# Nine more seven-product steps, state additions and rT on GpSimd, and a reordered head in a fused SSD and gated-cosine kernel

## The chip, the cores and the metric

The kernel runs on one core of one Trainium2 chip. The metric is the device time of one execution in microseconds (us). A core has five engines with a queue each, which run their own instructions in order and wait for one another by semaphores: TensorE (PE; its weight loads are shown as PEld), VectorE (DVE), ScalarE (ACT), GpSimd (POOL) and SyncE (SP), which here issues nearly all transfers. Matrix products go to PSUM; GpSimd works on SBUF alone in this kernel.

## The reference

Two stages, all in fp32. The first is a state-space scan (Mamba-2 SSD) over 4 sequences, 8 heads, 768 positions, head width D = 32 and state width N = 16. In chunks of positions:

```python
cum = cumsum(log(clip(a)))                      # within the chunk
L   = exp(cum_i - cum_j), causal
M   = (C_i . B_j) * L
y   = M @ x + (C_i . state) * exp(cum_i)
state = exp(sum(la)) * state + sum_j B_j x_j exp(cum_last - cum_j)
```

The second takes the result as 3072 tokens of width 256 through a gated layer of width 2048:

```python
h = x @ w_in          # 3072x256 @ 256x2048
g = h * cos(h)
out = g @ w_out       # 3072x2048 @ 2048x256
```

## The kernel before

**Blocks and steps.** Positions are cut into 6 blocks c of 128; two units of 64 positions make a block. The result of the scan for a block, yT, has 512 columns: 256 per unit u. The layer on top runs in 96 steps n, 16 per block (n = 16c + f). In blocks 1 to 5 steps f = 0 to 7 belong to unit 0 and f = 8 to 15 to unit 1; j counts the 8 pieces of the layer's width within a unit. A step consists of:

- the first product hp = yT x w_in on PE (`first`, line 672), 8 passes of 256 columns;
- `wind_k` (ACT, 679), `wind_w` (DVE, 685), `gate` (ACT sine, 694) and `gated` (DVE, 699), which make gT = h cos h out of hp;
- `differ` (GpSimd, 724 to 727): three operations that make the sums and differences gd of gT;
- the second product (`second`, `seven`, 848) into o, two steps later (LAG = 2).

The second product is done in Strassen-Winograd form from block 1 on: seven products of half size for eight, with operands gd and the prepared weight differences (`differ_w`). After the eight steps of a unit the seven partial sums are copied (`take`, ACT), added up and stored (`rest`, 873); `unsummed` spreads the four parts of that over four steps on GpSimd.

**Runs.** In some steps, the *runs*, the first product takes that form too (`first7`, 772): 7 products of two passes of 128 columns, i.e. 14 passes, in the order 1, 6, 7, 5, 4, 3, 2. It needs differences of y (`differ_y`, 754, four of them, i = 0 to 3, in the tile `yd`, which lies in `ms[2]`) and of w_in (`differ_in`, 743). Product 6 reads difference 2, products 5, 7 and 4 read differences 0, 1 and 3. Difference 2 is made of difference 0. The sums of a seven-product step are made on DVE (785 to 793), and `gated` of the step before a run stands behind the sums of its first step. Runs before: steps 41 to 45, 57 to 61 and 73 to 77 (f = 9 to 13 of blocks 2 to 4), and 81 to 93. PSUM for the running sums and one hp comes from the tag "scan", two buffers of two banks, which the scan also uses.

**The scan of a block.** It is laid out over the steps of the block before it, in the table `steps`: `reaches` (running products of a, 586), `turn_blocks` (a transpose on DVE, 594), `turn2` (ACT copies of C scaled, 603, and rT = C times reach, DVE, 605), `inner2` (products g, 615), `weights` (477), `add_state` (state of the block before, decayed and added, 510), `decays0` (running products for the block after next, 387), `open2` and `finish2` (the y products, 629 and 641), and ACT copies of y to yT (`take_y`). `differ_y` of unit 1 is made by GpSimd at f = 4, 5, 6, 6. In the loop over n the work of a step is recorded in the order: first product, wind, take_y, gate, the first item of the list `behind`, gated with differ, the rest of `behind`, differ_y, sums of the outputs, differ_in, second product, inner2. This order is the order in each engine's queue.

**The head.** Blocks 0 and the first units are done unit by unit (`inner`, `weights`, `finish0`, `reach0`, `weigh_c`). Up to the first product at 14.47 us C must be loaded (`load_c`, four transfers on ACT's queue), copied (358), transposed (407) and scaled (411); B transposed (421); a spread over heads (`spread_a`, 376) and scanned (387). hp 0 is done in two halves; between them stands the whole of `finish0(1)`: the rT products (527), the sums for the state (489) and the y products (537). The weights come in pieces as 32-bit words, are graded (`grade`: ACT 256, 258, GpSimd 259) and joined (`join`: DVE 271, 275, GpSimd 283).

## Time and profile before

| | |
|---|---|
| median of 3 runs | 364.44 us (363.73 to 365.11) |
| profiled execution | 364.44 us |
| its span, first to last instruction | 362.7 us |
| mean granted TensorE clock | 0.998 |
| L672, first products, 544 passes | 129.6 us, 382 ns each |
| L724, 726, 727, gd on GpSimd, 79 each | 735, 501, 493 ns |
| L754, differ_y on GpSimd, 128x128, 12 of them | 455 ns |
| L510, state additions on DVE, 28 of them | 419 and 754 ns |
| L605, rT on DVE, 8 of them | 507 ns |
| L586, reach scans on DVE, 32 of them | 368 ns |

The passes overlap each other, so the time of one pass (382 ns) is longer than the distance from one to the next. A line number is that of the kernel before; a tile's name stands left of the arrow, what it is made of on the right.

### The profile page before, as it was taken

Reading aid. Unit: us, or ns where it says so; the run is one execution under the profiler, and the core shown is the slowest. Engines: PE = TensorE matmul, PEld = TensorE weight load, DVE = VectorE, ACT = ScalarE, POOL = GpSimd, SP = SyncE. Lnnn points to the kernel's source line nnn. Section 1 sums busy time; section 2 is a strip of 40 time slices with the busy share of each in tenths; the row PEclk is TensorE's granted clock in tenths of the full one; section 3 lists DMA queues with packets and bytes.
Section 4 is the critical chain, followed back from the end, with each engine's and each line's share of the span. In section 5 each row is a group of like instructions: output and inputs, shape, how many; then the busy total and the mean of one; then the engine's idle time right before and its main releaser. Section 6 shows DMA issues by size and latency. Waiting matters only on the chain.

```text
span 362.7 us, 10240 instructions
## 1 busy us (share of the span) xinstructions
PE 357.0 (98%) x4070; PEld 326.0 (90%) x4070; DVE 276.0 (76%) x504; ACT 184.0 (51%) x352; POOL 239.7 (66%) x387
## 2 busy tenths in 40 slices
PE   8999999999999999999999999999999999999995
PEld 4788888889999999999989999999999999999995
DVE  7779998488876987878766877875776776688864
ACT  3597656544454346534536533545553544444552
POOL 5567767699666677674786666686666465475572
PEclk9999999999999999999999999999999999999999
DMA  7984997666583429113228202110001001001001
GB/s 138 246 284 141 189 196 122 85 125 98 134 129 58 99 51 135 14 34 76 53 53 119 23 3 75 28 33 11 0 2 31 0 3 33 0 3 29 3 17 44
DMA packets 96624, 26.43 MB, mean 73 GB/s; under 512 B 86624, under 2 KB 92480, under 8 KB 96576
## 3 DMA queue, kind: packets, MB, share of 16 engines
q1 hardware_dynamic: 95328, 25.38, 34.9%
q8 instruction: 32, 0.52, 0.6%
q10 hardware_dynamic: 1248, 0.39, 0.5%
q14 instruction: 16, 0.13, 0.1%
HBM read 22.36 MB, written 3.34 MB: 71 GB/s over the span
## 4 chain that ended last, share of the span: by engine, by line
PE 96%; DMA 2%; DVE 1%; issue 0%; ACT 0%; POOL 0%; DVEq 0%
PE o L848 35%; PE hp L672 33%; PE o L808 8%; PE m L772 7%; PE hp L772 5%; DMA bc<-in_C_dram 2%; PE y L641 2%; PE g L615 1%; PE y L489 1%; PE y L629 1%; PE g L468 1%; PE y L537 1%; PE y L527 1%; PE o L900 0%; PE tp L451 0%
## 5 line engine op out<-in xcount | busy, mean ns | idle before, releaser
L672 PE MATMUL hp<-yT,w_in 128*128 128x256 f32 x544 | 129.6, 382 | 0.1
L672 PEld LDWEIGHTS hp<-yT,w_in 128*128 128x128 f32 x544 | 99.0, 190 | 13.8 <-issue 1.4
L724 POOL TENSOR_TENSOR gd<-gT 128x256 f32<-128x256 f32 x79 | 58.1, 735 | 76.9 <-DVE gT L699 61.8
L694 ACT ACTIVATE w<-w,quarter 128x512 f32<-128x512 f32 x96 | 69.4, 723 | 65.8 <-DVE w L685 65.7
L685 DVE SCALAR_TENSOR_TENSOR w<-hp,k 128x512 f32<-128x512 f32 x96 | 65.8, 686 | 45.4 <-ACT k L679 45.2
L679 ACT ACTIVATE k<-hp 128x512 int32<-128x512 f32 x96 | 57.2, 596 | 68.6 <-PE hp L672 60.3
L699 DVE TENSOR_TENSOR gT<-hp,w 128x512 f32<-128x512 f32 x96 | 65.6, 683 | 12.2 <-ACT w L694 8.3
L848 PE MATMUL o<-words,gd 128*128 128x128 f32 x474 | 66.0, 275 | 0.0
L848 PEld LDWEIGHTS o<-words,gd 128*128 128x128 f32 x474 | 59.4, 192 | 0.0
L848 PE MATMUL o<-w_out,gT 128*128 128x128 f32 x316 | 50.4, 278 | 0.0
L848 PEld LDWEIGHTS o<-w_out,gT 128*128 128x128 f32 x316 | 45.4, 191 | 3.1
L726 POOL TENSOR_TENSOR gd<-gT,gd 128x128 f32<-128x128 f32 x79 | 39.6, 501 | 6.2
L727 POOL TENSOR_TENSOR gd<-gT,gd 128x128 f32<-128x128 f32 x79 | 39.0, 493 | 6.2
L848 PE MATMUL o<-w_out,gd 128*128 128x128 f32 x158 | 30.6, 276 | 0.0
L848 PE MATMUL o<-words,gT 128*128 128x128 f32 x158 | 30.6, 275 | 0.0
L808 PE MATMUL o<-w_out,gT 128*128 128x256 f32 x128 | 30.0, 380 | 0.0
L387 DVE TENSOR_TENSOR_SCAN lam<-arow,unit 128x512 f32<-128x512 f32 x20 | 29.9, 1496 | 0.1
L808 PEld LDWEIGHTS o<-w_out,gT 128*128 128x128 f32 x128 | 24.2, 190 | 3.6 <-POOL w_out L283 0.4
L848 PEld LDWEIGHTS o<-words,gT 128*128 128x128 f32 x158 | 24.0, 192 | 0.0
L848 PEld LDWEIGHTS o<-w_out,gd 128*128 128x128 f32 x158 | 24.0, 192 | 0.0
L772 PE MATMUL m<-m,words 128*128 128x128 f32 x168 | 23.4, 276 | 0.0
L772 PE MATMUL hp<-yT,w_in 128*128 128x128 f32 x112 | 21.7, 275 | 0.0
(130 smaller groups left out, 463.6 us busy)
## 6 DMA issues: line engine op xcount, KB each, us to landing
words<-in_moe_w_in_dram SPq DMA_DIRECT2D x8, 512.0 KB
words<-in_moe_w_out_dram SPq DMA_DIRECT2D x8, 512.0 KB
xr<-in_x_dram SPq DMA_DIRECT2D x24, 128.0 KB
arow<-a_cut SPq DMA_DIRECT2D x10, 256.0 KB
arow<-a_cut SPq DMA_DIRECT2D x10, 252.0 KB
out_dram<-sum SPq DMA_DIRECT2D x18, 128.0 KB
bc<-in_B_dram SPq DMA_DIRECT2D x24, 64.0 KB
blocks<-in_B_dram SPq DMA_DIRECT2D x16, 32.0 KB
```

The source lines that it names most:

```text
L387: V.tensor_tensor_scan(out=lams[k][:, p, hs].rearrange(flat), data0=rows_.rearrange(flat), data1=unit0[:, hs].rearrange(flat), initial=0.0 ...
L672: PE.matmul(to_[:, e], lhsT=w_in[:, k, fs], rhs=y[:, k], start=(k == 0), stop=(k == KT - 1), skip_group_check=True)
L679: ACT.activation(k, hp[n], AF.Copy, bias=0.25, scale=INV_2PI)
L685: V.scalar_tensor_tensor(out=w, in0=hp[n], scalar=INV_2PI, in1=k, op0=ALU.mult, op1=ALU.subtract)
L694: ACT.activation(cos, cos, AF.Sin, bias=quarter, scale=TWO_PI)
L699: V.tensor_tensor(out=gT[n], in0=hp.pop(n), in1=cos, op=ALU.mult)
L724: G.tensor_tensor(out=d[:, 0:2], in0=g[:, 1:2].to_broadcast([P, 2, P]), in1=g[:, 3::-3], op=ALU.subtract)
L726: G.tensor_tensor(out=d[:, 2], in0=g[:, 0], in1=d[:, 0], op=ALU.subtract)
L727: G.tensor_tensor(out=d[:, 3], in0=g[:, 2], in1=d[:, 2], op=ALU.subtract)
L772: PE.matmul(dst[q], lhsT=w[q], rhs=y_[q], start=(q in (6, 1, 7)), stop=True, skip_group_check=True)
L808: PE.matmul(o[c, u][:, t], lhsT=g[:, 2 * e + t], rhs=w_out[:, 2 * j + e], start=(j == e == t == 0), stop=(j == NJ - 1 and e == 1), skip_gr ...
L848: PE.matmul(at[q], lhsT=a_[q], rhs=w[q], start=(j == 0 and q in starts), stop=(j == NJ - 1), skip_group_check=True)
```

## The change

Runs are added at f = 2, 3, 4 of blocks 2, 3 and 4 (steps 34 to 36, 50 to 52, 66 to 68). The scan's work on DVE is moved away from these steps: reaches to f = 5 as two scans of 260 elements for eight of 64 (the rows are stored with a leading zero, `lead` starts each run of 65), the block transposes to the last step of the block before and f = 1, the first `decays0` from f = 2 to f = 0. rT becomes a function of its own, `scale2`, on GpSimd for blocks 3 to 5, and so does the state addition, `add_state2`, two operations for four. The copies of C (`turn2`) stay on ACT at f = 3 and 4. `differ_y` makes both units' differences at f = 0, 0, 1, 1 on GpSimd. The sums of the outputs keep out of f = 2 and 3 on GpSimd.

In the head the fourth C transfer goes to SP's queue behind the load of a; the copy of C is one GpSimd operation; C is transposed ahead of B; x of unit 1 is loaded ahead of the second weight piece; the first piece is joined in halves; in `finish0` of units 0 and 1 the sums stand ahead of the y products; half of g of unit 1 is done behind the first half of hp 0.

```diff
@@ load_c, loads @@
-    for b in range(NB):
-        load_c(b, nc.scalar)
+    for i in range(NB):
+        load_c(i, nc.scalar if i < NB - 1 else nc.sync)
...
-    fetch("in", 1)
     for s in range(2):
         load_x(1, s)
+    fetch("in", 1)
@@ join @@
+            if halves:
+                for f in (slice(0, P), slice(P, 2 * P)):
+                    G.tensor_tensor(out=dst[:, :, f].bitcast(U32), in0=bits[:, :, f],
+                                    in1=last[:, :, f], op=ALU.add)
+                return
@@ add_state, now beside it @@
+    def add_state2(k):
+
+        dec = scan.tile([P, 2, 2, 2 * D], FP32, tag="whole", bufs=1, name="whole")
+        flat = "p s q d -> p (s q) d"
+        G.tensor_tensor(out=dec.rearrange(flat), in0=after[k - 1].rearrange(flat),
+                        in1=reach[k // 2][:, :, k % 2, W:].to_broadcast([P, NB, 2 * D]),
+                        op=ALU.mult)
+        return lambda: G.tensor_tensor(out=after[k], in0=after[k], in1=dec, op=ALU.add)
@@ finish0 @@
+        if k < 2:
+            sums(k, at, strip, start=True)
+        if between:
+            between()
...
-        sums(k, [y[0][:, s, 3 * P:] for s in range(2)], lambda q, s: slice(32 * q, 32 * q + 32),
-             start=(k == 0))
+        if k > 1:
+            sums(k, at, strip)
@@ reaches @@
-    def reaches(c, b):
-        s, p = divmod(b, 2)
-        if p == 0:
-            reach[c, s] = scan.tile([P, 2, P], FP32, tag="reach", name="reach")
-        for k in range(2):
-            i = slice(k * W, (k + 1) * W)
-            V.tensor_tensor_scan(out=reach[c, s][:, p, i], data0=along[c][:, b, i],
-                                 data1=ones[:, 0:W], initial=1.0, op0=ALU.mult, op1=ALU.mult)
+    def reaches(c, s):
+        if s == 0:
+            reach[c] = scan.tile([P, NB, 2, W + 1], FP32, tag="reach", bufs=1, name="reach")
+        V.tensor_tensor_scan(
+            out=reach[c][:, 2 * s:2 * s + 2].rearrange("p b k i -> p (b k i)"),
+            data0=along[c][:, 2 * s:2 * s + 2].rearrange("p b i -> p (b i)"),
+            data1=lead.rearrange("p b i -> p (b i)"), initial=0.0, op0=ALU.mult, op1=ALU.add)
@@ turn2 @@
-        rT = scan.tile([P, 2, P], FP32, tag="rT", name="rT")
-        V.tensor_tensor(out=rT, in0=tp[:, 1], in1=reach[c, s], op=ALU.mult)
-        part[c, s] = (tp[:, 0], cT, rT)
+        part[c, s] = (tp[:, 0], cT)
+
+    def scale2(c, s, eng):
+        r2[c, s] = rT = scan.tile([P, 2, P], FP32, tag="rT", name="rT")
+        eng.tensor_tensor(out=rT.rearrange("p q (k i) -> p q k i", k=2),
+                          in0=turned.pop((c, s))[:, 1].rearrange("p q (k i) -> p q k i", k=2),
+                          in1=reach[c][:, 2 * s:2 * s + 2, :, 1:], op=ALU.mult)
@@ head, in order @@
     tp_b = bank([P, 4, P], "tp", "o")
+    take_c, of_c = turn_c()
+    take_c(0)
     turn_b(0, tp_b)()
-    ACT.copy(out=c0[:, 3:4].rearrange("p r h n -> p h r n"), in_=c4[:, :, 3:4])
...
-    join("in", 0)
+    c1 = copy_c(of_c)
+    join("in", 0, halves=True)
     decays0(1, 0, 1, 2)
+    yT0, take_s0, _ = finish0(0, lambda: spread_a(1, 1, tag="h"))
     decays0(1, 1)
-    take_s0, _ = finish0(0)
-    take_b = turn_b(1, tp_b)
+    weigh0(1)
+    turn_b(1, tp_b)()
     scan_reach = reach0(1)
     scan_reach()
-    take_b()
+    weigh_c(1, c1)
+    yT0()
     take_s0()
-    for t in range(2):
-        inner(1, t)
-    weigh0(1)
-    weigh_c(1, of_c)
+    inner(1, 0)
@@ first_steps @@
-        for q in range(2):
-            weights(1, q)
+        weights(1, 0)
         states_of = []
-        first(0, lambda: states_of.extend(finish0(1)))
+
+        def unit1():
+            inner(1, 1)
+            weights(1, 1)
+            states_of.extend(finish0(1))
+
+        first(0, unit1)
@@ steps @@
-             dict(reach=(1, 2), turn=(3, 4), inner=5, weigh=(6, 7), state=(0, 5),
-                  decays=(2, 8, 14, 15), along=(6, 7)) for c in range(2, NC)}
+             dict(reach=(5, 5), turn=(-1, 1), cut=(3, 4), scale=(6, 7), inner=5, weigh=(6, 7),
+                  state=(2, 8), decays=(0, 8, 14, 15), along=(6, 7)) for c in range(2, NC)}
@@ runs @@
-    runs = [*(range(NF * c + 9, NF * c + 14) for c in range(2, NC - 1)),
+    runs = [*(range(NF * c + f, NF * c + l) for c in range(2, NC - 1) for f, l in ((2, 5), (9, 14))),
             range(NC * NF - 15, NC * NF - 2)]
@@ the loop over n @@
-            for i, at in enumerate((4, 5, 6, 6) if 2 <= c < NC - 1 else ()):
+            for i, at in enumerate((0, 0, 1, 1) if 2 <= c < NC - 1 else ()):
                 if at == f:
-                    differ_y(c, i, G, slice(1, 2))
-            if unsummed and (c > 1 or summed[0]):
+                    differ_y(c, i, G)
+            for e, s in chunks_at(n, "scale"):
+                if e > 2:
+                    scale2(e, s, G)
+            for add in adds:
+                add()
+            adds[:] = [add_state2(2 * e - 1 + i) for e, i in chunks_at(n, "state") if e > 2]
+            if unsummed and (c > 1 and f not in (2, 3) or summed[0]):
```

More of the change, by code (lines that the diff above doesn't have):

```diff
@@ L77 @@
     along, blocks = {}, {}
-    ones = const.tile([P, P], FP32, name="ones")
-    V.memset(ones, 1.0)
+    lead = const.tile([P, NB, W + 1], FP32, name="lead")
     def fill(dst):
@@ L87, in fill @@
                   start=True, stop=True, skip_group_check=True)
-    a_all = dram.tile([NB, H, S], FP32, name="a_all")
+    a_all = dram.tile([NB, H, 2 * NC, W + 1], FP32, name="a_all")
     a_cut = dram.tile([NB, H, S], FP32, name="a_cut")
@@ L177, in load_unit_along @@
                 nc.sync.dma_start(
-                    out=alongs[k][:, 2 * p + s, 1:],
-                    in_=a_all[2 * s + p, :, k * W:(k + 1) * W].unsqueeze(1).to_broadcast([H, N, W]))
+                    out=alongs[k][:, 2 * p + s],
+                    in_=a_all[2 * s + p, :, k].unsqueeze(1).to_broadcast([H, N, W + 1]))
     def load_along(c, seqs=range(NB)):
@@ L185, in load_along @@
         if c not in along:
-            along[c] = rows.tile([P, NB, P], FP32, tag="along", bufs=2, name="along")
+            along[c] = rows.tile([P, NB, 2 * (W + 1)], FP32, tag="along", bufs=2, name="along")
         for b in seqs:
@@ L191, in load_along @@
                 nc.sync.dma_start(
-                    out=along[c][rs, b], in_=a_all[b, hs, c * P:(c + 1) * P].unsqueeze(1)
-                    .to_broadcast([hs.stop - hs.start, N, P]))
+                    out=along[c][rs, b], in_=a_all[b, hs, 2 * c:2 * c + 2]
+                    .rearrange("h k i -> h (k i)").unsqueeze(1)
+                    .to_broadcast([hs.stop - hs.start, N, 2 * (W + 1)]))
     a0 = const.tile([P, 2, W], FP32, name="a0")
@@ L200 @@
     ms = [scan.tile([P, 2 * H * W], FP32, tag=f"m{b}", bufs=1, name="m") for b in range(NB)]
-    lead, along1, reach1 = (ms[2][:, i * NB * (W + 1):(i + 1) * NB * (W + 1)]
-                            .rearrange("p (b i) -> p b i", b=NB) for i in range(3))
+    along1, reach1 = (ms[2][:, i * NB * (W + 1):(i + 1) * NB * (W + 1)]
+                      .rearrange("p (b i) -> p b i", b=NB) for i in range(1, 3))
     reachs = {1: reach1, 2: along1, 3: reach1}
@@ L264, in grade, with join @@
             return rest
-    def join(which, i, between=None):
+    def join(which, i, between=None, halves=False):
         parts = held.pop((which, i), ())
@@ L349 @@
     G.tensor_scalar(out=a0[:, 1], in0=a0[:, 1], **clip)
+    c0 = loads.tile([P, 2, 2, 4, 2, N], FP32, tag="blocks", name="c0").rearrange(
+        "p a b c d n -> p (a b c d n)").rearrange("p (r h n) -> p r h n", r=4, h=H)
+    G.tensor_copy(out=c0.rearrange("p r h n -> p h r n"), in_=c4)
     for p in range(2):
@@ L355 @@
                   in_=mine.unsqueeze(2).to_broadcast([P, H, N]))
-    c0 = loads.tile([P, 2, 2, 4, 2, N], FP32, tag="blocks", name="c0").rearrange(
-        "p a b c d n -> p (a b c d n)").rearrange("p (r h n) -> p r h n", r=4, h=H)
-    G.tensor_copy(out=c0[:, 0:3].rearrange("p r h n -> p h r n"), in_=c4[:, :, 0:3])
     G.memset(lead, 0.0)
@@ L431, in reach0, with copy_c, weigh_c @@
             data1=lead.rearrange(flat), initial=0.0, op0=ALU.mult, op1=ALU.add)
-    def weigh_c(k, of):
+    def copy_c(of):
         c = scan.tile([P, NB, W], FP32, tag="rT", name="c1")
-        of(k, c)
+        of(1, c)
+        return c
+    def weigh_c(k, c):
         rTs[k] = t = scan.tile([P, NB, W], FP32, tag="rT", name="rT")
@@ L508, in add_state, with finish0 @@
             for p in range(2):
-                i = k % 2 * W + W - 1
                 V.scalar_tensor_tensor(out=after[k][:, s, p], in0=after[k - 1][:, s, p],
-                                       scalar=reach[k // 2, s][:, p, i:i + 1],
+                                       scalar=reach[k // 2][:, 2 * s + p, k % 2, W:],
                                        in1=after[k][:, s, p], op0=ALU.mult, op1=ALU.add)
-    def finish0(k):
+    def add_state2(k):
[5 more added lines that the diff above has]
+        return lambda: G.tensor_tensor(out=after[k], in0=after[k], in1=dec, op=ALU.add)
+    def finish0(k, between=None):
         m, xk = m_of[k], xrs[k]
@@ L520, in finish0 @@
                for t in range(2) for s in range(2)]
+        at = [y[0][:, s, 3 * P:] for s in range(2)]
+        strip = lambda q, s: slice(32 * q, 32 * q + 32)
+        if k < 2:
+            sums(k, at, strip, start=True)
+        if between:
+            between()
         if k:
@@ L546, in finish0, with take_y @@
                 ACT.copy(out=t_[:, t].rearrange("p (s i) -> p s i", s=2), in_=y[t][:, :, 0:P])
-        else:
+        def take_y():
             ACT.copy(out=t_.rearrange("p t (s i) -> p s t i", s=2),
@@ L576, in add @@
             return exchange
-        return take, add
-    def reaches(c, b):
-        s, p = divmod(b, 2)
-        if p == 0:
-            reach[c, s] = scan.tile([P, 2, P], FP32, tag="reach", name="reach")
-        for k in range(2):
-            i = slice(k * W, (k + 1) * W)
-            V.tensor_tensor_scan(out=reach[c, s][:, p, i], data0=along[c][:, b, i],
-                                 data1=ones[:, 0:W], initial=1.0, op0=ALU.mult, op1=ALU.mult)
-    turned, ys = {}, {}
+        return (take, add) if k else (take_y, take, add)
+    def reaches(c, s):
[5 more added lines that the diff above has]
+            data1=lead.rearrange("p b i -> p (b i)"), initial=0.0, op0=ALU.mult, op1=ALU.add)
+    turned, ys, r2 = {}, {}, {}
     def turn_blocks(c, s):
@@ L598, in turn2 @@
     def turn2(c, s):
-        tp = turned.pop((c, s))
+        tp = turned[c, s]
         cT = scan.tile([P, 2, 2, P], FP32, tag="cT2", bufs=2, name="cT2")
@@ L612, in inner2 @@
                            for q in range(4)):
-            bT, cT, _ = part[c, s]
+            bT, cT = part[c, s]
             r, i = group(q, s), slice(k * W, (k + 1) * W)
@@ L629, in open2 @@
             PE.matmul(y[s][o_:o_ + W, q // 2, i:i + W], lhsT=after[2 * c + k - 1][r, s, p],
-                      rhs=part[c, s][2][r, p, k * W:(k + 1) * W], start=(k == p == 0), stop=False,
+                      rhs=r2[c, s][r, p, k * W:(k + 1) * W], start=(k == p == 0), stop=False,
                       tile_position=(r.start, o_), skip_group_check=True)
@@ L916 @@
     tp_b = bank([P, 4, P], "tp", "o")
+    take_c, of_c = turn_c()
+    take_c(0)
     turn_b(0, tp_b)()
-    ACT.copy(out=c0[:, 3:4].rearrange("p r h n -> p h r n"), in_=c4[:, :, 3:4])
     spread_a(0, 1, 1, 2, "h")
     decays0(0, 1, 1, 2)
-    take_c, of_c = turn_c()
     spread_a(1, 0, 0, 2, "h")
-    take_c(0)
     decays0(1, 0, 0, 2)
@@ L929 @@
     spread_a(1, 0, 1, 2, "h")
-    spread_a(1, 1, tag="h")
     for q in range(2):
@@ L933 @@
     take_c(1)
-    join("in", 0)
+    c1 = copy_c(of_c)
+    join("in", 0, halves=True)
     decays0(1, 0, 1, 2)
+    yT0, take_s0, _ = finish0(0, lambda: spread_a(1, 1, tag="h"))
     decays0(1, 1)
-    take_s0, _ = finish0(0)
-    take_b = turn_b(1, tp_b)
+    weigh0(1)
+    turn_b(1, tp_b)()
     scan_reach = reach0(1)
     scan_reach()
-    take_b()
+    weigh_c(1, c1)
+    yT0()
     take_s0()
-    for t in range(2):
-        inner(1, t)
-    weigh0(1)
-    weigh_c(1, of_c)
-    la = const.tile([RB, NU, P], FP32, name="la")
+    inner(1, 0)
+    la = const.tile([RB, NU, 2, W + 1], FP32, name="la")
     cut = const.tile([RB, NU, P], FP32, name="cut")
@@ L953, in clip_cut @@
         G.memset(cut[:, :, 0:1], 0.0)
-        store_a(a_cut, cut)
+        nc.sync.dma_start(
+            out=a_cut.rearrange("(u b) h (c p) -> (b h c) u p", u=NU, p=P), in_=cut)
     def clip_all():
-        G.tensor_scalar(out=la, in0=a_in, **clip)
-    def store_a(dst, src):
-        nc.sync.dma_start(
-            out=dst.rearrange("(u b) h (c p) -> (b h c) u p", u=NU, p=P), in_=src)
+        G.memset(la[:, :, :, 0:1], 0.0)
+        G.tensor_scalar(out=la[:, :, :, 1:], in0=a_in.rearrange("p u (k i) -> p u k i", k=2), **clip)
     piece = {n: ("in", (n + 3) // 2) if n % 2 else ("out", n // 2) for n in range(NF)}
@@ L978, in rest_of_loads @@
     def rest_of_loads():
-        store_a(a_all, la)
+        nc.sync.dma_start(
+            out=a_all.rearrange("(u b) h (c k) i -> (b h c) u (k i)", u=NU, k=2),
+            in_=la.rearrange("p u k i -> p u (k i)"))
         load_arow(2)
@@ L1002, in rest_of_loads @@
                 load_b(k, s)
-    steps = {c: dict(reach=(5, 6), turn=(6, 7), inner=8, weigh=(9, 10), state=(-NF, 12),
-                     decays=(8, 11, 13, 14), along=(12, 13)) if c == 2 else
-             dict(reach=(1, 2), turn=(3, 4), inner=5, weigh=(6, 7), state=(0, 5),
-                  decays=(2, 8, 14, 15), along=(6, 7)) for c in range(2, NC)}
+    steps = {c: dict(reach=(5, 6), turn=(6, 7), cut=(7, 8), scale=(7, 8), inner=8, weigh=(9, 10),
+                     state=(-NF, 12), decays=(8, 11, 13, 14), along=(12, 13)) if c == 2 else
+             dict(reach=(5, 5), turn=(-1, 1), cut=(3, 4), scale=(6, 7), inner=5, weigh=(6, 7),
+                  state=(2, 8), decays=(0, 8, 14, 15), along=(6, 7)) for c in range(2, NC)}
     first_decays = (NF + 1, NF + 2, NF + 3, NF + 4)
@@ L1030 @@
     AHEAD = 4
-    runs = [*(range(NF * c + 9, NF * c + 14) for c in range(2, NC - 1)),
+    runs = [*(range(NF * c + f, NF * c + l) for c in range(2, NC - 1) for f, l in ((2, 5), (9, 14))),
             range(NC * NF - 15, NC * NF - 2)]
     sevens = {n: r for r in runs for n in r}
-    late, at_ = [], {}
+    late, at_, adds = [], {}, []
     def first_of_seven(n):
@@ L1046, in first_of_seven @@
             at_["hp"] = bank([P, TB], "hp", "o")
-        to_ = at_["hp"] if i % 3 == (n > NF * (NC - 1)) else bank([P, TB], "hp", "h")
+        run = sevens.get(n, sevens.get(n - 1))
+        to_ = at_["hp"] if i % 3 == (len(run) != 5) else bank([P, TB], "hp", "h")
         if n not in sevens:
@@ L1110 @@
     add_s, rests_of = first_steps()
-    for k in (2, 3):
-        G.memset(alongs[k][:, :, 0:1], 0.0)
     rest_of_loads()
@@ L1144 @@
                 take_y(0)
-            for e, s in chunks_at(n - 1, "turn"):
+            for e, s in chunks_at(n, "cut"):
                 turn2(e, s)
+            for e, s in chunks_at(n, "scale"):
+                if e == 2:
+                    scale2(e, s, V)
             for k in units_at(n, 2):
@@ L1162 @@
             weighed = [k for k, p in decays_at(n) if p and k != 5 and k < 2 * NC - 1]
-            behind += [lambda k=2 * c - 1 + i: add_state(k) for c, i in chunks_at(n, "state")]
-            behind += [lambda c=c, b=2 * s + p: reaches(c, b) for c, s in chunks_at(n, "reach")
-                       for p in range(2)]
+            behind += [lambda k=2 * c - 1 + i: add_state(k) for c, i in chunks_at(n, "state")
+                       if c == 2]
+            behind += [lambda c=c, s=s: reaches(c, s) for c, s in chunks_at(n, "reach")]
             behind += [lambda at=at: turn_blocks(*at) for at in chunks_at(n, "turn")]
@@ L1193 @@
                     differ_y(NC - 1, i, V)
-            for i, at in enumerate((4, 5, 6, 6) if 2 <= c < NC - 1 else ()):
+            for i, at in enumerate((0, 0, 1, 1) if 2 <= c < NC - 1 else ()):
                 if at == f:
-                    differ_y(c, i, G, slice(1, 2))
-            if unsummed and (c > 1 or summed[0]):
+                    differ_y(c, i, G)
+            for e, s in chunks_at(n, "scale"):
+                if e > 2:
[4 more added lines that the diff above has]
+            if unsummed and (c > 1 and f not in (2, 3) or summed[0]):
                 unsummed[0](range(summed[0], summed[0] + 1), G)
```

## The prediction

> **What bounds the kernel now.** I read the page first: busy time and the chain that ended last. TensorE (PE) is busy 98% of the span and the chain is PE for 96%, so until the profile shows a gap, a microsecond that PE waits is a microsecond of the whole.

> ```profile
> PE 357.0 (98%) x4070; PEld 326.0 (90%) x4070; DVE 276.0 (76%) x504; ACT 184.0 (51%) x352; POOL 239.7 (66%) x387
> ...
> PE 96%; DMA 2%; DVE 1%; issue 0%; ACT 0%; POOL 0%; DVEq 0%
> ```

> Next the chain in order of time (start, us, what). It prices a step of each kind.

> ```profile
> 164.14 1.56 PE o L848 x14
> 165.92 0.89 PE m L772 x8
> 167.26 1.56 PE o L848 x14
> 169.05 0.89 PE m L772 x8
> 170.39 1.71 PE o L848 x14
> 172.33 0.89 PE m L772 x8
> 173.67 1.56 PE o L848 x14
> ...
> 194.89 1.73 PE hp L672 x8
> 196.62 1.56 PE o L848 x14
> 198.18 1.73 PE hp L672 x8
> ```

> An ordinary step is 1.73 + 1.56 = 3.29 us. Steps of the five-step run are 167.26 - 164.14 = 3.12, then 3.13, then 3.28 (its second product took 1.71), then 3.12 and 3.13. PE is the clock of every stage; other engines matter only where they deliver late.

> Last the timeline around step 48, the first of block 3, where the change puts new work (start, us, engine, line, operation; in brackets idle time and what ended it).

> ```profile
> 191.43 1.89 PE L672 MATMUL hp<-yT,w_in 128*128 128x256 f32 x8
> ...
> 193.42 0.60 ACT L679 ACTIVATE k<-hp 128x512 int32<-128x512 f32 x1 [0.64 <-PE hp L672]
> ...
> 194.05 0.69 DVE L685 SCALAR_TENSOR_TENSOR w<-hp,k 128x512 f32<-128x512 f32 x1 [2.06 <-ACT k L679]
> ...
> 194.66 0.95 DVE L510 SCALAR_TENSOR_TENSOR state<-state,reach 128x64 f32<-128x64 f32 x4
> ...
> 195.60 0.69 DVE L699 TENSOR_TENSOR gT<-hp,w 128x512 f32<-128x512 f32 x1
> ...
> 196.44 0.73 POOL L724 TENSOR_TENSOR gd<-gT 128x256 f32<-128x256 f32 x1 [1.50 <-DVE gT L699]
> ...
> 197.25 0.46 POOL L726 TENSOR_TENSOR gd<-gT,gd 128x128 f32<-128x128 f32 x1
> ...
> 197.78 0.46 POOL L727 TENSOR_TENSOR gd<-gT,gd 128x128 f32<-128x128 f32 x1
> ...
> 198.01 1.89 PE L672 MATMUL hp<-yT,w_in 128*128 128x256 f32 x8
> ...
> 198.20 0.46 POOL L743 TENSOR_TENSOR words<-w_in,words 128x128 f32<-128x128 f32 x1
> ...
> 201.24 1.39 DVE L387 TENSOR_TENSOR_SCAN lam<-arow,unit 128x512 f32<-128x512 f32 x1
> ```

> It shows that gT of step 48 is there 4.9 us after its first product began, that GpSimd's three differences of it end at 198.23, and that the first product of step 50 begins at 198.01. Two steps' distance is thus just used up by one gate and its gd.

> **Part 1, nine more seven-product steps.** Steps 34 to 36, 50 to 52 and 66 to 68 go from 3.29 to run steps. By the chain above three such steps are 3.12 + 3.13 + 3.28 = 9.53 against 9.87: -0.34 a run, **-1.0** for three.

> **Part 2, the differences of y (`differ_y`).** A run needs them for its unit. So far GpSimd makes unit 1's at steps 4, 5 and 6 of the block, long before step 9. Now it makes both units' at steps 0 and 1, and the run begins at step 2. In the built order GpSimd's queue there is: gd of step 0, differences 0 and 1, one `differ_in` piece (blocks 3 and 4), differences 2 and 3, then gd of step 1. PE's second product of step 2 (number 6) reads difference 2. PE runs in order, so all behind it waits.

> When is difference 2 there? The change also moves the scan of `decays0` from step 2 to step 0, ahead of gT, in the place of the state additions (0.95). Block 3: 194.66 + 1.39 (scan, row of 201.24) = 196.05; gT 0.69, 196.74; gd starts 0.15 later and takes 198.23 - 196.44 = 1.79, 198.68. A difference of both units is 128x256; the nearest row is gd's first, 0.73 long, and such operations follow each other about 0.7 apart: two give 200.1, the piece 0.46 gives 200.55, difference 2 another 0.73, 201.3. PE is ready at 198.01 + 0.22 (a product is two of a step's 14 passes, 1.57/7) = 198.23. Wait **3.05**.

> Block 4 the same way: product 66 would begin at 254.90, ready 255.12; w of step 64 is at 250.94, scan from 251.55, so 252.94, gT 253.63, gd 255.57, two differences 257.0, a 128x256 piece (0.73) 257.7, difference 2 at 258.45. Wait **3.3**.

> Block 2: ready at 141.18 + 0.22 = 141.40. w of step 32 begins at 137.56, the scan may go from 138.17, but GpSimd works on gd of step 31 from 138.11. A scan that met a GpSimd operation took 2.45 instead of 1.39:

> ```profile
> 131.07 2.45 DVE L387 TENSOR_TENSOR_SCAN lam<-arow,unit 128x512 f32<-128x512 f32 x1
> ```

> Held until 138.84 it ends at 140.23; gT 140.9, gd from 141.05 to 142.85, three differences 145.0: wait **3.6** (2.95 if the scan is not held; I take the held one, because the overlap is in the row). Sum **+9.95**. Ends: differences as fast as the 128x128 rows (0.46) give 7.5; if each run also loses 1.13 (VectorE's two block transposes, moved to step 1) in the same place, 13.3.

> What is late next: gT of step 1 stands behind the run's sums on VectorE. From difference 2 PE has six products (1.35), a second product (1.56) and a first one (1.57) to do, 4.5 us, before it wants gd of step 1; the sums end 1.4 after it (behind product 4, 0.98, and an addition of 0.43), gT takes 0.69 and gd 1.9, 4.0. Hidden by 0.5; where the cover goes, as in the 3.28 of the old run, it is the 0.15 already counted.

> **Part 3, work moved to GpSimd.** Per block two rT (0.7 each) and two state additions (two operations of 0.73 each). VectorE loses eight additions and two rT; PE waited for none of them, so that gives nothing. GpSimd can take it: gd of 48 ended 198.23 and PE wants it at 199.74, 1.5 us of cover. If steps 53 to 56 eat the cover (two gd in step 53, then rT, sum and sc0 together), each block loses up to 0.7: 0 to 2.1 in all, and I take **0**. Reaches as two scans instead of eight, and rows stored with their leading zero (same issue count): VectorE and SP off the path, 0.

> **Part 4, the head.** The last C transfer now goes second on SP's queue. It was issued at 2.99, after a wait, and took 3.89; the copy of C on GpSimd began at 6.93. Issued near 1.2 it lands between 3.4 (the 2.23 of the C transfers of 0.74) and 5.1 (its old 3.89). With the copy (0.51 for three quarters, so 0.68) C is ready by 5.8 at the latest, and its transposes begin when PE has done the three spreads, at 6.33 instead of 7.49. B goes behind it, and the transposes (0.66), the scaled copies (0.84) and the copy of B (0.37) end at 8.2 instead of 9.03: 0.8 gained at g of unit 0. Then x of unit 0 must be there (sums used it at 11.22, never seen waiting), y's products start at about 10.9 instead of 11.49, 0.6. Behind that the first half of hp 0 now waits for yT, which is copied after B of unit 1; sums lie ahead of the rT products, which waited 0.33 on GpSimd's rT. I take the second half of hp 0 from 17.67 to 17.2, **-0.5**; ends 0 (x or B late by the reordered queue) and -0.9. In(1) comes later: its join ended 18.48, its first use is near 20.3, which covers 1.3 us of delay.

> **Part 5, the granted clock.** The last products ended at 358.86. Windows behind them (stretch, length, busy of PE, PEld, DVE, ACT, POOL, granted clock, DMA):

> ```profile
> 358.90:361.40 2.50, 0.00 (x0) 0.00 (x0) 0.41 (x1) 0.00 (x0) 0.00 (x0) 1.00 0.42 105
> 361.60:362.60 1.00, 0.00 (x0) 0.00 (x0) 0.00 (x0) 0.00 (x0) 0.00 (x0) 0.50 0.00 0
> ```

> About 2.6 us after the last product the clock is halved. All three waits are longer, so PE may come out of them slow. No row shows this in mid kernel. Price: at the start two passes of 128x256 (a_ps, from 3.46) took 1.16, and two from 6.60 took 0.60, so slow time lasted at most 5.8 us from the first product at 0.77, a loss of up to 2.9; so 0 to 8.7 for three. I take half the waits and half the price, 3 x 0.5 x 1.45 = **+2.2**. [...]

> **Sum.** The profiled execution took 364.44 (span 362.7 and 1.7 around it), and 364.44 is also the median of the three. 364.44 - 1.0 + 9.95 + 0 - 0.5 + 2.2 = **375.1 us**.

> **Rivals.**
> - *The waits without the clock* (no. 1): 375.1 - 2.2 = 372.9. For it: PE never stands for 2.5 us in the trace before 358, so nothing proves a closing. Against: 0.50 behind the last product.
> - *Not slower* (no. 2): the differences are in time. One mechanism: GpSimd reaches difference 2 before product 6 in all three runs; it decides from 198.2, not 201.3. Then 364.44 - 1.0 - 0.5 = 362.9, and with the head's best end 362.5. For it: GpSimd is idle 1.50 before gd of 48. Against: that gd stands ahead in its queue, and its gT can't come sooner than k, w and Sin (2.9 us behind hp).
> - *GpSimd becomes the bound of steps 0 to 8* (no. 3): nine gd (15.5), four differences (2.9), rT and additions (4.4), sums (2.4), sc0 and pieces (2) are 27 us of some 31. With port conflicts like that of 131.07 (1.1 each), one or two a step pair, it passes that: 1 to 2 us a block on top, about 380.
> - *Short waits* (no. 4): yT lands, but differences overlap or run near 0.46 and the scan is cheap: 1.5 us a run, 364.44 - 1.5 + 4.5 = 367.5.

> **How the numbers follow.** Forecast 0.50, no. 1 0.27, no. 3 0.10, no. 4 0.08, no. 2 0.05. Range 370.5 to 379.5: from 372.9 less the 2.4 between 9.95 and 7.5, to three closings at 2.2 each, midway between 1.45 and 2.9 (6.6 for the 2.2 in all, +4.4). It leaves out nos. 2 and 4 and most of no. 3. About 0.5% (1.8 us) can be told from no change. Faster 0.03 and same 0.03 come from no. 2 and a little of no. 4, slower 0.94 from the rest.

> **What would show it.** In the profile after: PE idle of 3 to 3.6 us before the second product of steps 34, 50 and 66, ended by GpSimd's `differ_y`; about 1.0 less PE time in the nine steps; hp 0's second half near 17.2; a granted clock under 1 behind the waits. No gap at step 50 makes the prediction wrong; so would gaps spread over every step.

## The result, and the profile after

The changed kernel takes 378.64 us (median of 5 runs, 377.97 to 379.62) against 364.44 (5 runs, 363.73 to 365.11): ratio 1.0398, 95% interval 1.0383 to 1.0412, slower by 14.2 us. The profiled execution took 379.62 with a span of 377.8 and a mean granted clock of 0.986 (before 362.7 and 0.998).

The page of after: the span, the busy line of PE, the granted clock in 40 slices, and the chain that ended last by engine.

```profile
span 377.8 us, 10363 instructions
...
PE 362.9 (96%) x4124; PEld 332.2 (88%) x4124; DVE 273.9 (72%) x485; ACT 185.2 (49%) x360; POOL 256.8 (68%) x405
...
PEclk9999999999999998999999899999899999999999
...
PE 78%; POOL 6%; DVE 5%; SPq 3%; issue 3%; ACT 2%; DMA 1%; DVEq 0%; ACTq 0%; POOLq 0%
```

The chain is no longer all PE (96% before): GpSimd and VectorE now stand in it. The clock row has three dents. PE is busy 5.9 us longer though it has less to multiply, and idle some 9 us longer. Both point at the same places, as the waits of PE show (us in total, times, longest):

```profile
PE m L799 <- POOL m L781: 7.9, 3, 2.7
PE hp L699 <- DVE gT L726: 0.9, 1, 0.9
...
PE hp L699 <- POOL w_in L288: 0.5, 1, 0.5
```

Line 799 is a run product, line 781 is `differ_y`: three waits, one a block. The timeline of GpSimd and then of PE around the first, step 34 (start, us, engine, line):

```profile
142.12 0.73 POOL L751 TENSOR_TENSOR gd<-gT 128x256 f32<-128x256 f32 x1
142.93 0.45 POOL L753 TENSOR_TENSOR gd<-gT,gd 128x128 f32<-128x128 f32 x1
143.46 0.45 POOL L754 TENSOR_TENSOR gd<-gT,gd 128x128 f32<-128x128 f32 x1
143.87 1.40 POOL L781 TENSOR_TENSOR m<-yT 128x256 f32<-128x256 f32 x2
145.24 1.53 POOL L781 TENSOR_TENSOR m<-yT,m 128x256 f32<-128x256 f32 x2
...
142.90 0.39 PE L799 MATMUL hp<-yT,w_in 128*128 128x128 f32 x2
146.01 1.04 PE L799 MATMUL m<-m,words 128*128 128x128 f32 x6 [2.73 <-POOL m L781]
```

GpSimd first makes the gd of step 32, then the four differences, each some 0.73. PE has issued product 1 at 142.90 and can't issue product 6 before difference 2 ends at 146.0. Start to start the two products are 3.11 apart here, 2.94 and 3.00 in blocks 3 and 4, against 0.22 where nothing waits: 2.89 + 2.72 + 2.78 = 8.4 us.

Now the windows from the wait on (stretch, length, busy of PE, PEld, DVE, ACT, POOL, granted clock, DMA):

```profile
143.30:146.71 3.41, 0.70 (x6) 0.70 (x6) 0.42 (x1) 1.18 (x4) 3.25 (x6) 1.00 0.96 136
146.71:150.12 3.41, 3.41 (x18) 3.35 (x17) 1.95 (x5) 0.00 (x0) 0.43 (x2) 0.50 0.43 72
```

In the 3.41 us that end shortly after the wait PE was busy for 0.70; in the next 3.41 it has half the clock. The first four passes of a second product take 0.85 there, from their start at 148.26 to the next pass, and 0.44 behind it, from 152.28. So PE does in the stretch what takes half the time otherwise and loses 1.7 (an estimate: half of 3.41). The same follows the other two waits, from 208.15 and 269.59. Three such stretches make 5.1, with the waits 13.5. By the start of each second product against the trace of before, the runs of steps 34 to 36, 50 to 52 and 66 to 68 cost 4.4, 4.1 and 4.1 us, 12.6 in all: waits and halved stretches, less what the run steps save.

This execution is the slowest of the five. Its wait of 0.9 for gT comes at 84 us, behind a scan that waited for a transfer of `arow`; the other traces with this head don't have it. The mean granted clock is 0.986 in three of the five executions and 0.991 in two. Three halved stretches give 0.986 here and two give 0.991 in e8_warm1 below, so it seems that in two executions one wait passed without a halved stretch.

### The profile page after: what moved, and what is told of

Same layout as the page of the kernel before. It is cut to its first block, busy times and chain, and to the rows that moved or that the text cites. A ratio compares the mean times of both kernels' runs of the same rounds, so it can differ in the third digit from the quotient of the medians.

```text
span 377.8 us, 10363 instructions
## 1 busy us (share of the span) xinstructions
PE 362.9 (96%) x4124; PEld 332.2 (88%) x4124; DVE 273.9 (72%) x485; ACT 185.2 (49%) x360; POOL 256.8 (68%) x405
## 4 chain that ended last, share of the span: by engine, by line
PE 78%; POOL 6%; DVE 5%; SPq 3%; issue 3%; ACT 2%; DMA 1%; DVEq 0%; ACTq 0%; POOLq 0%
PE o L875 30%; PE hp L699 20%; PE m L799 9%; PE hp L799 7%; PE o L835 4%; SPq L150 2%; POOL m L781 2%; PE g L642 1%; PE y L668 1%; PE a_ps L381 1%; DVE gT L726 1%; POOL gd L751 1%; SPq L107 1%; DVE w L712 1%; DVE sum L900 1%
## 5 line engine op out<-in xcount | busy, mean ns | idle before, releaser
L699 PE MATMUL hp<-yT,w_in 128*128 128x256 f32 x472 | 112.7, 383 | 1.5 <-DVE gT L726 0.9
L699 PEld LDWEIGHTS hp<-yT,w_in 128*128 128x128 f32 x472 | 85.9, 190 | 14.2 <-DVE gT L726 1.4
L726 DVE TENSOR_TENSOR gT<-hp,w 128x512 f32<-128x512 f32 x96 | 65.7, 685 | 15.0 <-ACT w L721 11.1
L875 PE MATMUL o<-words,gd 128*128 128x128 f32 x474 | 68.1, 281 | 0.3 <-issue 0.3
L875 PEld LDWEIGHTS o<-words,gd 128*128 128x128 f32 x474 | 61.3, 197 | 0.9 <-issue 0.5
L875 PEld LDWEIGHTS o<-w_out,gT 128*128 128x128 f32 x316 | 46.0, 197 | 2.6
L799 PE MATMUL m<-m,words 128*128 128x128 f32 x222 | 31.4, 278 | 7.9 <-POOL m L781 7.9
L812 DVE TENSOR_TENSOR m<-m 128x128 f32<-128x128 f32 x37 | 10.8, 292 | 36.9 <-PE m L799 33.3
L799 PEld LDWEIGHTS m<-m,words 128*128 128x128 f32 x222 | 27.7, 192 | 8.7 <-POOL m L781 8.5
L806 ACT COPY m<-hp 128x128 f32<-128x128 f32 x37 | 9.7, 261 | 41.5 <-PE hp L799 41.5
L799 PE MATMUL hp<-yT,w_in 128*128 128x128 f32 x148 | 29.4, 281 | 0.0
```

The source lines that it names most:

```text
L699: PE.matmul(to_[:, e], lhsT=w_in[:, k, fs], rhs=y[:, k], start=(k == 0), stop=(k == KT - 1), skip_group_check=True)
L726: V.tensor_tensor(out=gT[n], in0=hp.pop(n), in1=cos, op=ALU.mult)
L799: PE.matmul(dst[q], lhsT=w[q], rhs=y_[q], start=(q in (6, 1, 7)), stop=True, skip_group_check=True)
L875: PE.matmul(at[q], lhsT=a_[q], rhs=w[q], start=(j == 0 and q in starts), stop=(j == NJ - 1), skip_group_check=True)
```

## The experiments

Twelve kernels were run. Times are medians; each ratio is against runs of the kernel before made beside it (364.03 to 364.26 in the three batches). A granted clock or a wait quoted from one is of its profiled execution.

### 1. The differences in time (e1_early)

```diff
+            if 2 <= c < NC - 1 and f == 0:
+                for i in range(4):
+                    differ_y(c, i, G, slice(0, 1))
             if n + 1 in sevens or n in sevens:
                 late.append(n)
...
-            for i, at in enumerate((0, 0, 1, 1) if 2 <= c < NC - 1 else ()):
+            for i, at in enumerate((4, 5, 6, 6) if 2 <= c < NC - 1 else ()):
                 if at == f:
-                    differ_y(c, i, G)
+                    differ_y(c, i, G, slice(1, 2))
```

> The differences of unit 0 are recorded on GpSimd at step 0 of blocks 2 to 4, ahead of that step's gate product and words; those of unit 1 go back to steps 4, 5, 6 and 6. Theory A (the wait itself and the halved clock that follows it are the loss: 2.89 + 2.72 + 2.78 = 8.4 us of waits and 3 x 1.7 = 5.1 us of clock): in blocks 3 and 4 product 6 no longer waits and no half-clock stretch follows, some 4.2 us back each; block 2 may keep a wait of 1 to 1.5 us, since GpSimd still has its first words differences ahead, but too short for a half-clock stretch. Time 366 to 368. Rival B (GpSimd's load is the bound: the work it took on only moves the wait somewhere else): the waits come back on another value of GpSimd (gd or words) and the time stays above 373.

Measured: 365.97 us, ratio 1.005 (1.0035 to 1.0066). The mean clock is 0.998 and no stretch is halved before the end. GpSimd, then PE, at step 50:

```profile
195.50 1.80 POOL L781 TENSOR_TENSOR m<-yT 128x128 f32<-128x128 f32 x2
197.25 0.99 POOL L781 TENSOR_TENSOR m<-yT,m 128x128 f32<-128x128 f32 x2
198.21 0.73 POOL L751 TENSOR_TENSOR gd<-gT 128x256 f32<-128x256 f32 x1
...
198.73 0.39 PE L799 MATMUL hp<-yT,w_in 128*128 128x128 f32 x2
198.96 0.83 PE L799 MATMUL m<-m,words 128*128 128x128 f32 x6
```

The four differences of one unit end at 198.24, before product 1 begins, because they stand ahead of gd and need nothing but yT. Product 6 follows 0.23 behind product 1. Of the three waits 0.2 us is left, in block 2 (1 to 1.5 was expected there):

```profile
PE m L799 <- POOL m L781: 0.2, 1, 0.2
```

That 1 to 1.5 is too short for a halved stretch was the author's estimate, which this run doesn't test; in e9 below three waits of at most 1.1 left the mean clock at 0.999.

Theory A holds. GpSimd makes as many elements as in the changed kernel, so rival B, its load, is out as a cause of the 12.7 us that this edit gives back. The edit changes two things: unit 0's differences stand further ahead in the queue, and unit 1's are no longer made with them. The second alone would take some 0.8 off each wait (an estimate from the rows: three operations of 0.46 ahead of product 6 for three of 0.73). So most of the gain is the place in the queue; no run took the two apart.

### 2. The clock alone (e2_warm, e8_warm1)

```diff
-        for q in (1, 6):
-            product(q)
+        product(1)
+        if n in (2 * NF + 2, 3 * NF + 2, 4 * NF + 2):
+            for _ in range(4):
+                PE.matmul(at_["m"][:, 1, 1:4].rearrange("p q m -> p (q m)"),
+                          lhsT=nc.const_aps.tensor(1.0, (P, P), FP32),
+                          rhs=nc.const_aps.tensor(1.0, (P, 3 * P), FP32),
+                          start=True, stop=True, skip_group_check=True)
+        product(6)
```

e8_warm1 has one such product (`range(1)`).

> Four products of 128x384 whose results nothing reads are put between products 1 and 6 of steps 34, 50 and 66, so TensorE works in the stretch in which it waited; everything else, the wait for difference 2 included, stays. The four should take about 2.1 us at the rate of the six 128x128 products in 1.04 us, so product 6 starts when it did. Theory A (the half clock after each wait costs 1.7 us): the granted clock stays at 1 after the waits and the time falls by about 5.1, to 373 to 374. Rival C (the low granted clock beside the waits is only how the trace shows them, the loss is the waits and what GpSimd holds up behind them): no change, 378 to 379.

> As e2_warm, with one product (128x384, about 0.5 us) instead of four before product 6 of steps 34, 50 and 66; its result is read by nothing. Where e2_warm kept the full clock with some 2 us more of work in each wait, this asks how little does. If any work in the stretch keeps the clock: no half-clock stretch, 373 to 375. If the stretch is judged by how much of it TensorE was idle (2.2 to 2.4 of 3.4 us then): half-clock stretches of 3.41 us after some or all waits, and 377 to 379 with all three.

e2_warm: 373.71 us, ratio 1.0262 (1.0241 to 1.0284), 4.93 below the changed kernel. PE at step 34:

```profile
142.83 0.39 PE L799 MATMUL hp<-yT,w_in 128*128 128x128 f32 x2
143.06 2.76 PE L807 MATMUL m<-const-float32-1.0 128*128 128x384 f32 x8
```

The four products took 2.76, not 2.1, and product 6 began at 145.95, 3.12 behind product 1 as before: the wait is there, filled with work that nobody reads, and the clock stays at 1, as the window behind it shows:

```profile
146.00:149.40 3.40, 3.40 (x29) 3.34 (x30) 1.91 (x5) 0.00 (x0) 0.73 (x2) 1.00 0.75 92
```

So the halved stretches cost 4.9 us, or 4.5 when each kernel is set against the kernel before of its own batch (14.20 and 9.68 above it): 1.5 to 1.6 for each of three, and more for each if two of the executions had only two. Half of 3.41 is 1.7. Rival C is out. What e2 still has over e1, 373.71 - 365.97 = 7.7, is the price of the waits.

e8_warm1: 376.44 in one run. Two of three stretches are halved. Its windows:

```profile
143.65:147.06 3.41, 2.18 (x18) 2.12 (x19) 0.71 (x2) 0.00 (x0) 1.90 (x3) 1.00 0.77 92
201.68:205.09 3.41, 1.52 (x10) 0.91 (x9) 0.88 (x2) 1.64 (x4) 3.33 (x6) 1.00 0.78 88
205.09:208.50 3.41, 3.41 (x18) 3.40 (x17) 1.94 (x5) 0.00 (x0) 0.43 (x2) 0.50 0.33 78
```

The wait of step 50 falls into one window, busy for 1.52 of 3.41, and the next window is halved. The wait of step 34 is as long (2.09) but lies across a border of windows, 143.65, which is 61.44 ahead of 205.09; the window that holds more of it leaves 2.18 busy, and the clock stays at 1. So one such product in the wait did not keep the clock in each case here. In these rows it stayed where the window was busy for 2.18 and fell where it was busy for 1.52 and 1.45, as the second expectation has it in kind. The last section has cases that PE's busy time alone doesn't part.

### 3. The load without the runs (e4_no_new_runs, e12_schedule)

```diff
-    runs = [*(range(NF * c + f, NF * c + l) for c in range(2, NC - 1) for f, l in ((2, 5), (9, 14))),
+    runs = [*(range(NF * c + f, NF * c + l) for c in range(2, NC - 1) for f, l in ((9, 14),)),
```

e12_schedule has this and the old head (experiment 4).

> Only the first halves of the nine new run steps go back to full products; the new head, the state additions and rT on GpSimd, and the differences recorded at steps 0 and 1 all stay. Theory A (the new runs' waits and clock cost 12.6 of the 14.2 us, net of their gain): 365.8 to 366.4, with no half-clock stretch before the end. [...]

> No new run steps and the head of the kernel before: what is left of the change is its schedule (scans of two rows at once, transposes and states at other steps) with state additions and rT on GpSimd. Theory F (the head makes the 1.1 to 1.3 us that e4_no_new_runs lies above the kernel before): 364.0 to 364.5, no difference from the kernel before. Rival B (GpSimd's added work costs by itself): 365.0 to 365.6.

e4: 365.36 us, 1.0034 (1.0019 to 1.005). e12: 364.49 us, 1.0008 (0.9998 to 1.0018), not to be told from the kernel before. So the state additions, rT, the wider scans and the moved transposes cost nothing, and what e4 has over e12, 0.9 us (1.1 when each is set against the kernel before of its batch), is the new head. e12 lies where theory F had it, e4 0.4 below the 365.8 that theory A expected at least.

### 4. The head (e3_old_head, e6_early_old_head, e7_early_in1)

```diff
-    for i in range(NB):
-        load_c(i, nc.scalar if i < NB - 1 else nc.sync)
+    for b in range(NB):
+        load_c(b, nc.scalar)
...
+    fetch("in", 1)
     for s in range(2):
         load_x(1, s)
-    fetch("in", 1)
...
-        if k < 2:
-            sums(k, at, strip, start=True)
...
-    join("in", 0, halves=True)
+    join("in", 0)
```

e3 puts the whole head of before under the changed kernel, e6 under e1_early; e7 is e1_early with only the load of the second weight piece, `fetch("in", 1)`, moved back.

> The head of the kernel before (order of loads, first C tile in two parts, one hp 0), with the new run steps kept. Theory A (the head is worth little: it was 0.2 ahead at the second half of hp 0 and 0.45 behind at the third second product, and the 1.2 us wait of the scan for arow at 84 us came with SP's queue drifting, which began in the head): if the drift comes from the later load of w_in's second piece, both go and the time is 376.9 to 377.2. Rival D (the drift comes from the new run steps' work or from elsewhere): only the 0.45 goes, 378.1 to 378.3. Rival E (the new head pays as the change says): the time rises by 0.5 or more, to 379 and above.

> The early differences of e1_early together with the head of the kernel before. e1_early took 365.97, e4_no_new_runs 365.36, both some 1.3 to 1.9 above the kernel before, though their profiled executions were their fastest. Theory F (what is left of the loss is the new head: w_in's second piece is loaded behind two x tiles, its words were taken up 1.3 to 2.9 us later in the traces, and in some executions TensorE waits for it): 364.2 to 364.8. Rival G (it is GpSimd's added work or the earlier steps of the schedule): 365.7 to 366.3 as with the new head.

> As e1_early with the new head, but the load of w_in's second piece is put back ahead of the two x tiles of pair 1, where the kernel before has it. Theory F1 (that one move in SP's queue is the head's whole loss): as e6_early_old_head or a little less, 363.9 to 364.8. Rival F2 (the x tiles, now later, are waited for by the y products instead, or C's loads ahead of B's are the cause): 365.5 or more.

e3: 377.07 us, 1.0373 (1.0337 to 1.0409). e6: 365.17 us, 1.0025 (1.0012 to 1.0037). e7: 364.92 us, 1.0033 (1.0015 to 1.005). Against their partners with the new head that is 1.6, 0.8 and 1.05 less; the intervals of e1 and e6 meet, and so do those of the changed kernel and e3, so only the difference of e4 and e12 stands clear, and these three agree with it in sign. e3 lies where its theory A had it, but the wait at 84 us that this theory counts is in the trace of after alone, so the agreement is in part luck. e6 is between theories F and G: the head is a part of what was left, not all. e7 lies between F1 and F2. In the trace the second weight piece is taken up by ScalarE at 13.95 before:

```profile
13.95 0.71 ACT L258 ACTIVATE mag<-words 128x512 f32<-128x512 f32 x1
```

and with the new head at 16.00, behind a wait for its transfer:

```profile
16.00 0.67 ACT L258 ACTIVATE mag<-words 128x512 f32<-128x512 f32 x1 [2.14 <-DMA words<-in_moe_w_in_dram]
```

In the profiles of after, e2 and e8 PE then waits 0.5 for the third weight piece, ahead of the first product of step 4 (at 27.70 in after), and in e2 0.4 more for the second piece, ahead of step 2. In those of e1 and e4 it waits for neither. e7 shows why the move back is no cure: its nine runs lie at 364.6 to 365.2 (six) and at 366.6 to 366.7 (three, two of them with a mean clock of 0.995), and the profile is one of the latter, with PE waiting for x:

```profile
PE y L497 <- DMA xr<-in_x_dram: 1.6, 2, 1.1
```

The window of that wait, 7.29 to 10.70, has PE busy for 1.77, and the next is halved. So rival F2 is there in some executions: with the other head edits in place, x or a weight piece came late in these traces in either order. How the kernel before gets both in time was not taken apart; it has C's loads, the copy of C and the sums in another order as well.

### 5. The kernel before with the runs alone (e9_runs_early)

```diff
-    runs = [*(range(NF * c + 9, NF * c + 14) for c in range(2, NC - 1)),
+    runs = [*(range(NF * c + f, NF * c + l) for c in range(2, NC - 1) for f, l in ((2, 5), (9, 14))),
...
+            if 2 <= c < NC - 1 and f == 0:
+                for i in range(4):
+                    differ_y(c, i, G, slice(0, 1))
...
-            if unsummed and (c > 1 or summed[0]):
+            if unsummed and (c > 1 and f not in (2, 3) or summed[0]):
```

The lines that give a run of three its banks came over as well.

> The kernel before with nothing but the nine new run steps and the early differences of unit 0: head, state additions, rT and schedule are those of before. Theory H (the run steps save 0.16 each where nothing waits, 1.4 in all, and about 0.3 a block goes again where GpSimd or VectorE is late): 363.2 to 364.0. Rival I (state additions and rT have to leave VectorE first, since VectorE has four additions more in each run step): steps 34 to 36, 50 to 52 and 66 to 68 wait for VectorE's sums, and the time is above 365.

Measured: 371.8 us, 1.023 (1.0195 to 1.0266). The waits of PE:

```profile
PE g L615 <- ACT cT L603: 3.2, 3, 1.1
...
PE o L848 <- POOL gd L726: 0.9, 2, 0.4
...
PE m L772 <- DVE hp L790: 0.7, 2, 0.4
```

Rival I holds in its time, and only in part in its place. The sums are waited for twice, 0.7 in all. The larger wait, 1.1 a block, is for cT: the block transposes (1.15 and 1.11 us on VectorE) stand in the steps of the run, w comes behind them, and ScalarE copies cT behind that. By the start of the second products blocks 2 and 3 lose 3.0 us each from step 35 (51) to step 38 (54); block 4 loses 2.0 there and 1.0 already at step 64. Leaving VectorE's work where it was costs 371.8 - 365.2 = 6.6 us against e6; taking it away buys no time alone (e12), but makes room for the runs.

### 6. What the runs are worth (e10_rT_vector, e11_two_runs)

```diff
-                    scale2(e, s, G)
+                    scale2(e, s, V)
```

and in e11 also

```diff
-    ... for c in range(2, NC - 1) for f, l in ((2, 5), (9, 14))),
+    ... for c in range(2, NC - 1) for f, l in ((2, 5), (9, 14))[c == 2:]),
...
-            if 2 <= c < NC - 1 and f == 0:
+            if 2 < c < NC - 1 and f == 0:
```

Both stand on e6_early_old_head.

> e6_early_old_head with the products rT of blocks 3 to 5 back on VectorE; the state additions stay on GpSimd. In e6 and e1 the run of three gains 0.49 in each block and about 0.55 goes again in the old run of five, where GpSimd comes to gd 0.8 us late (rT, the sums of the finished unit and sc stand ahead of it). Theory J (GpSimd's backlog behind the new run eats the gain): rT off GpSimd takes some 1.3 us of it, the old runs lose nothing in blocks 2 and 3, 364.2 to 364.8. Rival K (VectorE is as full there): no change, 365.0 to 365.4.

> e10_rT_vector with the new run steps in blocks 3 and 4 only; steps 34 to 36 of block 2 are full products again and unit 0's differences of block 2 are left out. Block 2 is where GpSimd has three quantities at once ahead of the run (words differences, sc, the differences) and i still loses 0.5 before the run and gains 0.5 in it. Theory J: no loss from leaving block 2's run, 364.0 to 364.6, a version at the level of the kernel before. Rival K: 365 as in e6.

e10: 364.97 us, 1.0024 (1.0006 to 1.0041), not to be told from e6. GpSimd ahead of step 41's gate, in e6:

```profile
167.50 0.68 POOL L621 TENSOR_TENSOR rT<-turned,reach 128x256 f32<-128x256 f32 x1
168.14 0.46 POOL L890 TENSOR_TENSOR sum<-ps,sum 128x128 f32<-128x128 f32 x1
168.55 0.64 POOL L398 TENSOR_TENSOR sc<-bc,lam 128x256 f32<-128x256 f32 x1
169.15 0.62 POOL L522 TENSOR_TENSOR whole<-state,reach 128x256 f32<-128x256 f32 x1
169.73 0.73 POOL L741 TENSOR_TENSOR gd<-gT 128x256 f32<-128x256 f32 x1
```

and in e10:

```profile
168.86 0.72 POOL L741 TENSOR_TENSOR gd<-gT 128x256 f32<-128x256 f32 x1 [0.48 <-PE o L865]
```

gd comes 0.9 sooner and doesn't stand in a queue any more, yet block 2 loses nearly as much as before (0.69 for 0.86, from step 33 to step 47): theory J is right on the backlog and wrong on what it costs.

e11: 363.73 us, 0.9983 (0.9971 to 0.9995), 0.5 below the kernel before beside it, and below the range that either theory gave. Leaving the run of block 2 out gives 1.24 us. By the start of each second product against the trace of before, a run step saves 0.16 in every block where nothing waits, and e10 loses 0.43 at the first step of block 2's run (e11 0.08) and, behind that run, 0.58 up to step 47, two steps behind the run of five (e11 0.12). Blocks 3 and 4 lose less than they gain: e11 lies 0.76 below e12 with its two runs, though rT and the place of the differences differ between them too.

## Why the prediction was right, and where it was off

The forecast, 375.1 with slower at 0.94, had the right mechanism and place, and the time lies in its range, near the upper end. The medians follow one another, each with one cause taken away. They come from four batches, in which the kernel before took 364.03 to 364.44, so a price between two batches is uncertain by up to 0.4.

| step | us | price of it | forecast |
|---|---|---|---|
| changed kernel | 378.64 | | |
| clock kept (e2_warm) | 373.71 | halved clock 4.9 | +2.2 |
| differences early (e1_early) | 365.97 | waits 7.7 | +9.95 |
| old head (e6_early_old_head) | 365.17 | head 0.8 | -0.5 |
| no new runs (e12_schedule) | 364.49 | runs 0.7 | -1.0 |
| kernel before beside it | 364.26 | load and schedule 0.2 | 0 |

That the sum is only 3.5 off is in part luck: the waits came 2.2 lower than forecast, the clock, the head and the runs 2.7, 1.3 and 1.7 higher.

- **Part 2, the waits.** Right in kind and number, 8.4 in the trace against 9.95. Block 3 came to 2.72 for 3.05; its scan took 1.25 and not 1.39. Block 4 came to 2.78 for 3.3. The sum has a scan ahead of gT there which isn't in either kernel: the last scan of this kind begins at 246.6 in before and at 257.0 in after, both ahead of step 64. What held gT was ScalarE's sine. Block 2 came to 2.89 for 3.6. The sum let its scan, held up, end 2.06 behind its start, and it took 1.76; besides, product 1 came 3.89 behind w of step 32, for 3.62 in before.

```profile
139.62 1.76 DVE L392 TENSOR_TENSOR_SCAN lam<-arow,unit 128x512 f32<-128x512 f32 x1
263.42 0.69 DVE L726 TENSOR_TENSOR gT<-hp,w 128x512 f32<-128x512 f32 x1 [0.86 <-ACT w L721]
```

- **Part 5, the clock.** This is the term that moved the forecast most from the result. It took half the waits at 1.45; in the profiled execution all three were followed by a halved stretch, and their price was 4.5 to 4.9. At 1.7 for each of three, half of a stretch of 3.41, the sum would have been 372.9 + 5.1 = 378.0. PE did not stand idle through the 3.41 us ahead of these falls of the clock: windows in which it was busy for 0.70 to 1.77 were followed by half the clock. The trace of before shows that at its end, in the window whose end is the fall of the clock that the prediction saw:

```profile
358.09:361.51 3.42, 0.75 (x4) 0.33 (x2) 0.98 (x3) 0.00 (x0) 0.00 (x0) 1.00 0.30 77
```

PE was busy for 0.75 of it: the wait ahead of this fall didn't fill the window. Rival no. 1 (waits without the clock, 372.9) is e2_warm's 373.71, and did not happen.
- **Part 3, GpSimd's load.** 0 was right for the load without the runs: e12 can't be told from the kernel before. Rival no. 3, GpSimd as the bound near 380, had a time close to the result and the wrong cause, as e1 shows with the same load. The stretch that it priced, an operation that takes longer beside one of the other engine, is in the traces again: in after the gd of 192.42 took 1.25 instead of 0.46 beside the scan of 191.98, and PE didn't wait for it; in e1 a difference pair of 0.9 took 1.80, at 195.50. No run shows what the two engines have in common there; "port" is the prediction's word for it.
- **Part 4, the head.** Wrong in sign. The first half of hp 0 came 1.0 sooner (13.49 for 14.47) and the second half 0.24 (17.43 for 17.67), half of the forecast. The step that failed is "In(1) comes later: ... covers 1.3 us of delay" (by its own figures, 20.3 less 18.48, it is 1.8). Its words were taken up 2.05 later and its join began at 18.71 for 17.21; in after it just came in time, in e2 PE waited for it, and the piece behind it was late as well. e4 against e12 gives +0.9. What else of the head costs time was not taken apart.
- **Part 1, the gain.** 0.16 a step was there, 0.49 a run. It was given back around the run of block 2, and for the most part in all of e6 and e10. With two runs e11 is 0.76 below e12.
- Rivals no. 2 and no. 4 fell with the waits.

What stays open: why e10 loses 0.43 at the first step of block 2's run. Its trace shows the wait: product 6 of step 34 comes 0.56 behind product 1 instead of 0.22, for difference 2. GpSimd's gd ahead of the differences takes 1.26 instead of 0.46 beside VectorE's scan (as in e1, 1.25 at 138.78 beside the scan of 138.01), but it takes 1.25 in e11 too, where without the run 0.08 is lost; so the stretch seems to cost only where the differences stand behind it. No run took that apart.

## What to carry to other kernels

Where an engine runs its queue in order, a value that needs only old data belongs ahead of one that waits for the running step; here the place of four small operations was worth most of 12.7 us, and their load without the runs nothing that can be measured. In the profiles of after and e8 five of six waits of TensorE of 1.9 to 2.7 us had a second price behind them in the clock (1.5 to 1.7 for each, against 2.6 for the wait itself in after); ask for it in the same step of the sum. Price a gain of 0.3 us a block against the work that it pushes together, and keep it only in the blocks that have room.

## What the runs showed of the hardware

PE's busy time doesn't part the two kinds sharply. e4 ends with a window of 1.47, less than the 1.52 and 1.77, and the clock stays at 1 behind it, as it does in after behind 2.04 (371.99 to 375.40).

```profile
357.56:360.97 3.41, 1.47 (x7) 0.95 (x5) 1.62 (x5) 0.00 (x0) 0.00 (x0) 1.00 0.25 55
360.97:362.80 1.83, 0.00 (x0) 0.00 (x0) 0.00 (x0) 0.00 (x0) 0.00 (x0) 1.00 0.17 40
```

So of the whole windows given here each of 1.45 us or less was followed by half the clock, and none of 2.04 or more. What decides between the two no run shows.
